# A segment-recurrent attention and its gradients: forward steps regrouped, V's rows moved by DMA, partial sums added by a matmul

## The chip, the cores and the metric

The kernel runs on one core of a Trainium2 chip. The core has a matrix engine (TensorE, PE in the profile; its weight loads are PEld), a vector engine (VectorE, DVE), a scalar engine (ScalarE, ACT), GpSimd (POOL) and a queue engine (SyncE, SP) that issues DMAs; SPq and POOLq are the DMA-issuing sides of SP and POOL. Engines run their own instruction streams in order and wait for one another by semaphores. The metric is the device time of one execution in microseconds, the median of several runs.

## The reference

The reference is a transformer block and its gradient. x is 2048 tokens of 448 numbers. The attention works through 64 segments of 32 tokens. Ahead of each segment stand 8 memory rows, which are the attention's own output for the 8 memory rows of the segment before, so segment s+1 can't start before segment s has ended:

```python
mem = mem0                                       # 8 x 448
for s in range(64):
    h = concat([mem, xs[s]])                     # 40 x 448
    q, k, v = h @ Wq, h @ Wk, h @ Wv             # 16 heads of 256
    scores = q @ k.T * scale                     # 40 x 40 per head, masked
    p = softmax(scores)
    o = (p @ v) @ Wo                             # 40 x 448
    mem = o[:8]; outs.append(o[8:])
h = x + concat(outs)                             # xs is layernorm(x)
h2 = h + (silu(n(h) @ w_gate) * (n(h) @ w_up)) @ w_down
```

The kernel returns h2 and the gradients for x, mem0, the four attention weights and the three weights of the feed-forward part. The gradient runs the recurrence backward: the gradient of `mem` goes from segment s+1 to s.

## The kernel before

The program has four stages, one after the other: a forward loop over the 64 segments (`forward_chain`), the feed-forward part with its own gradient (`ffn_phase`), a backward loop over the 64 segments (`backward_chain`), and the weight gradients (`tail_phase`). The order of instructions on each engine is the order in which the Python code states them (`manual_schedule`); no planner moves anything. Tiles wait for one another by the regions that they read and write.

**A segment's tokens.** Four segments make a tile of 128 rows. In each segment, only 32 of the 40 rows depend on the chain: the 8 memory rows and 24 of the segment's own. The other 8 of its own are computed for four segments at once in side units (`b_units` for k, q and v of the next tile, `o_units` for the output product of the tile before). The side units are cut into pieces (u1, e1, u2, u3, e3, ut, et) that stand between the pieces of the chain: `cur` is this segment's unit, `late` and `late2` hold the rest of the units of the two segments before. In every fourth segment (r = 0) `cur` is an output unit, in the others a projection unit.

**A projection** (`proj`, L468) multiplies 32 rows by 512 columns of weights, for four column groups at a time: the result of group g stands in partitions 32g to 32g+31 of one PSUM bank, 4 x 4 matmuls for a half of all columns. Kev, Qev and Vev are the copies in SBUF, [128, 1024], the first 512 columns being half 0. The evacuations alternate between DVE (`V`, L431) and ACT (`A`, L434). K and Q are then transposed (`tr_half`, L474) into kT and qT, which `scores` (L505) multiplies into two PSUM banks, s_ps0 and s_ps1, one for each half of the heads. The mask is put there ahead by a matmul (`mask_mm`, L488).

**V in rows.** P V needs V with the 40 tokens in partitions. `v_shift` copies 32 rows of each group from Vev to V_sb: DVE does half 0 and two groups of half 1, POOL (L731) the other two. The 8 rows of the side units come by DMA (`v_b_rows`, L646). V_sb holds heads 0 to 7 in partitions 0 to 39 and heads 8 to 15 in partitions 64 to 103. V_sb is stored to HBM as Vtok (L777) for the backward loop; K and Q are stored at L706 and L719.

**Softmax** runs on DVE and ACT, half by half: max (L738), subtract (L740), Exp (L742), sum (L745), reciprocal (L747), multiply into P_sb (L748). Meanwhile TensorE runs u1 and u2 of the side unit and the `spin` matmuls (L847), whose result is not used. `p_turn` (L761) transposes P head by head, 16 times 40x40; two copies, one on DVE and one on ACT, bring it to PT. Then 32 matmuls of P and V (L792), copies into oA and oB, 64 matmuls with Wo (`wo_mm`, L583) into four partition groups: group g holds a partial sum of one half of the 448 columns.

**The turn.** ACT copies the partial sums to `part`, two f32 transposes (L513) turn it, and a DVE reduce over the groups (`gsum`, L518) adds two partial sums per token and writes the next segment's memory rows into hA. A second reduce writes the segment's own rows to aT. The next segment's first projection waits for hA.

**The backward loop** ends its segment in the same way: `part` (copied half by ACT, half by DVE), a `turn` of four f32 transposes (L1207) and a `gsum` of four partial sums per token (L1212) into dA, the input of the next segment's projection. Once in four segments the side unit's partD is turned too, right behind it.

Of the kernel before, what the change touches and what calls it, by code (L numbers as in the profile page):

```python
# [15 lines left out]
P = 128  # L16
# [166 lines left out]
def run_all(k: _K):  # L183
# [38 lines left out]
    k.ident, k.identf = ident, identf  # L222
    eps_t = const.tile([P, 1], FP32)
# [38 lines left out]
    P_all = dram.tile([NSEG, 64 + L, H // 2 * L], BF16, name="P_all")  # L262
# [10 lines left out]
    with tc.tile_pool(name="wfwd", bufs=1) as wf, \  # L273
# [25 lines left out]
        with tc.tile_pool(name="workA", bufs=2) as work, tc.tile_pool(name="stageA", bufs=1) as stage:  # L299
# [22 lines left out]
            mv1 = small.tile([P, NT, 2], FP32, name="mv1", bufs=1)  # L322
# [58 lines left out]
    if True:  # L381
# [4 lines left out]
        if True:  # L386
            with tc.tile_pool(name="psB", bufs=6, space=bass.MemoryType.PSUM) as psb, \
# [6 lines left out]
                k.part = stage.tile([P, DP], FP32, name="partC")  # L394
                k.partB = stage.tile([P, DP], FP32, name="partD")
# [11 lines left out]
def forward_chain(k: _K, hA, NWIN, Wq_sb, Wk_sb, Wv_sb, Wo_sb, maskr, work, stage, ff):  # L407
# [27 lines left out]

    def slot(s):
        return s % NWIN
# [56 lines left out]
    def hsel(x, half):  # L494
        return x[0:NR].rearrange("p (a b i) n -> p a b i n", a=2, b=2)[:, :, half, :, :]
# [14 lines left out]
    def turn(src):  # L510
        y = ps1(FP32)
        for j in range(2):
            nc.tensor.transpose(y[0:DB, j * P:(j + 1) * P], src[:, j * DB:(j + 1) * DB], identf[:, :])  # L513
        return y[0:DB, 0:2 * P].rearrange("p (c b n) -> p c n b", c=KC, b=2)

    def gsum(out, in_):
        with nc.allow_low_precision("four float32 partial sums of one token"):
            nc.vector.tensor_reduce(out=out, in_=in_, axis=AX.X, op=ALU.add)  # L518
# [11 lines left out]
    def b_units(t, which):  # L530
# [6 lines left out]

        def u1():
            st["p0"] = ps1(FP32)
            proj(st["p0"], W_sb, stat, 0)  # L540
# [6 lines left out]
        def u2():  # L547
            st["p1"] = ps1(FP32)
            proj(st["p1"], W_sb, stat, 1, range(0, 2))

        def u3():
            proj(st["p1"], W_sb, stat, 1, range(2, 4))
# [33 lines left out]
    def o_units(t):  # L586
# [27 lines left out]
        def et():  # L614
            for kc in range(KC):
                gsum(T.aT[0:DB, kc, :].rearrange("p (r j) -> p r j", r=4)[:, :, XA:SEG],
                     st["y"][:, kc, :, :].rearrange("p (r i) g -> p r i g", r=4))
# [30 lines left out]

    def v_shift(V_sb, Vev, half, gs, eng):
# [15 lines left out]
    nc.gpsimd.memset(V_sb[:], 0.0)  # L665
    mask_mm(0)
# [4 lines left out]
    for s in range(NSEG):  # L671
# [19 lines left out]
        kT = work.tile([P, MC, L], BF16, name="kT", bufs=2)  # L691
        qT = work.tile([P, MC, L], BF16, name="qT", bufs=2)
# [13 lines left out]
        nc.sync.dma_start(out=dr["KtokA"][s], in_=Kev[:])  # L706
        pv0 = ps1()
        proj(pv0, Wv_sb, stat, 0)
        A(Vev[:, 0:HB], pv0[:, :])
# [3 lines left out]
        A(fm_view(kT, 0, 0, SEG), tr_half(Kev, 0))  # L713
        v_shift(V_sb, Vev, 0, (0, 1), V)
# [9 lines left out]
        pv1 = ps1()  # L724
        proj(pv1, Wv_sb, stat, 1, range(0, 2))
        A(fm_view(qT, 1, 0, SEG), tr_half(Qev, 1))
        proj(pv1, Wv_sb, stat, 1, range(2, 4))
        scores(qT, kT, 0)
        scores(qT, kT, 1)
        A(Vev[:, HB:GF], pv1[:, :])  # L730
        v_shift(V_sb, Vev, 1, (0, 1), lambda out, in_: nc.gpsimd.tensor_copy(out=out, in_=in_))  # L731
# [3 lines left out]
        P_sb = work.tile([P, HG, L], BF16, name="P_sb", bufs=2)  # L735
        for half in range(2):
# [5 lines left out]
            nc.scalar.activation(out=E_sb[0:NR, half], in_=S_sb[half][0:NR], func=ACT.Exp, scale=k.scale)  # L742
        for half in range(2):
# [8 lines left out]
        cur["u2"]()  # L752
        PT = work.tile([P, HG, L], BF16, name="PT", bufs=2)
        ppt = [ps1(BF16), ps1(BF16)]

        def p_turn(half):
            for gg in range(2):
                b = QB * gg
                for hh in range(HG):
                    if (hh // 2) % 2 == half:  # L760
                        nc.tensor.transpose(ppt[gg][b:b + L, hh * L:(hh + 1) * L], P_sb[b:b + L, hh, :], ident[b:b + L, b:b + L])  # L761
# [8 lines left out]
        for gg, eng in ((0, V), (1, A)):  # L770
            b = QB * gg
            eng(PT[b:b + L], ppt[gg][b:b + L, 0:HG * L].rearrange("p (h n) -> p h n", n=L))
        v_shift(V_sb, Vev, 1, (2, 3), V)
# [8 lines left out]
        for half in range(2):  # L782
            for gg in range(2):
                b = QB * gg
                po = ps1()
                i = 0
                for g in (2 * gg, 2 * gg + 1):
                    for j in range(4 * half, 4 * half + 4):
                        c = g * NJ + j
                        hh = c // DC - HG * gg  # L790
                        lc = c * P - gg * 2 * GF
# [1031 lines left out]
```

## Time and profile before

| | us |
|---|---|
| median of 3 runs | 3095.26 |
| lowest, highest | 3066.39, 3104.03 |
| profiled execution | 3067.6 |
| its span, first to last instruction | 3065.8 |
| forward loop, P V matmuls first to last | 70.6 to 1025.9 |
| backward loop, its products with dO first to last | 1402.4 to 2352.1 |

The busy time of an engine is the time in which it has an instruction of its own running; TensorE's matmuls overlap, so its busy time isn't its peak. A row of the timeline gives start, duration, engine, source line, operation, written tile `<-` read tiles, shape and count; what stands in brackets is the idle time before it and what ended it. The line numbers are those of the kernel before.

### The profile page before, as it was taken

Reading aid. Unit: us, or ns where it says so; the run is one execution under the profiler, and the core shown is the slowest. Engines: PE = TensorE matmul, PEld = TensorE weight load, DVE = VectorE, ACT = ScalarE, POOL = GpSimd, SP = SyncE. Lnnn points to the kernel's source line nnn. Section 1 sums busy time; section 2 is a strip of 40 time slices with the busy share of each in tenths; the row PEclk is TensorE's granted clock in tenths of the full one; section 3 lists DMA queues with packets and bytes.
Section 4 is the critical chain, followed back from the end, with each engine's and each line's share of the span. In section 5 each row is a group of like instructions: output and inputs, shape, how many; then the busy total and the mean of one; then the engine's idle time right before and its main releaser. Section 6 shows DMA issues by size and latency. Waiting matters only on the chain.

```text
span 3065.8 us, 108383 instructions
## 1 busy us (share of the span) xinstructions
PE 2825.9 (92%) x46532; PEld 1540.9 (50%) x46568; DVE 1546.5 (50%) x4123; ACT 1175.4 (38%) x3023; POOL 738.1 (24%) x1384
## 2 busy tenths in 40 slices
PE   3999999999999699995999999999998999989999
PEld 1555555555555355552555555555554454444454
DVE  4566666666655477772655566556554112211221
ACT  2444444444444356562444444444443111101110
POOL 1222222222222122221222222223222222223332
PEclk7999999999999899997999999999999999999999
DMA  8333333333333773348566566555566999999996
GB/s 262 101 103 114 114 104 108 119 104 105 107 119 99 200 181 116 117 133 188 138 183 154 143 177 158 143 169 171 138 158 197 309 222 197 197 204 208 195 208 135
DMA packets 612448, 482.84 MB, mean 157 GB/s; under 512 B 482944, under 2 KB 526544, under 8 KB 602432
## 3 DMA queue, kind: packets, MB, share of 16 engines
q1 hardware_dynamic: 565632, 289.17, 43.6%
q0 software_dynamic: 46336, 186.74, 18.3%
q8 instruction: 366, 6.00, 0.8%
q14 instruction: 114, 0.93, 0.1%
HBM read 135.08 MB, written 219.52 MB: 116 GB/s over the span
## 4 chain that ended last, share of the span: by engine, by line
PE 75%; issue 6%; DMA 5%; DVE 5%; ACT 5%; SPq 2%; POOL 1%; POOLq 0%; ACTq 0%; DVEq 0%
PE psf L468 14%; PE psf L1669 12%; PE psf L1200 10%; PE psf L1173 4%; PE psf L583 4%; PE psf L1474 3%; PE psf L1654 3%; PE psf L978 3%; PE psh L474 3%; ACT dO_sb L1167 2%; PE psf L1682 2%; PE psf L1061 2%; DMA wall<-in_A_Wv_dram 2%; PE s_ps L847 1%; PE pob L1200 1%
## 5 line engine op out<-in xcount | busy, mean ns | idle before, releaser
L468 PE MATMUL psf<-wall,hA 112*32 112x512 bf16 x6144 | 379.3, 381 | 17.0 <-DVE hA L518 15.2
L1669 PE MATMUL psf<-wall,H_all 128*128 128x512 bf16 x1404 | 320.9, 381 | 13.1 <-DMA wall<-dKA 11.0
L1669 PEld LDWEIGHTS <-H_all 128*128 128x128 bf16 x1440 | 139.5, 98 | 178.2 <-issue 21.2
L468 PEld LDWEIGHTS <-hA 112*32 112x32 bf16 x6144 | 140.5, 96 | 163.8 <-DVE hA L518 31.3
L1581 DVE CAST resc<-psf 128x512 bf16<-128x512 f32 (+1 forms) x58 | 39.1, 673 | 317.4 <-PE psf L1669 283.3
L731 POOL COPY V_sb<-Vev 32x512 bf16<-32x512 bf16 x128 | 77.6, 606 | 341.0 <-PE s_ps L505 329.9
L1579 ACT CAST resc<-psf 128x512 bf16<-128x512 f32 (+1 forms) x54 | 31.0, 574 | 329.0 <-PE psf L1669 291.6
L1525 POOL COPY dmem<-dA 128x32 bf16<-128x32 bf16 x63 | 13.3, 211 | 553.8 <-DVE dA L1212 553.8
L468 PE MATMUL psf<-wall,hB 112*32 112x512 bf16 x1536 | 105.6, 397 | 32.8 <-DMA wall<-in_A_Wk_dram 13.4
L1164 DVE COPY partC<-psf 128x224 f32<-128x224 f32 x64 | 25.1, 392 | 219.6 <-ACT partC L1167 219.6
L1173 PE MATMUL psf<-wall,dA 128*32 128x512 bf16 x2048 | 123.4, 383 | 13.0 <-DVE dA L1212 13.0
L1654 PEld LDWEIGHTS <-wall 128*128 128x128 bf16 x864 | 84.3, 99 | 90.4 <-issue 12.6
L1654 PE MATMUL psf<-dOut_all,wall 128*128 128x448 bf16 x640 | 125.7, 355 | 3.3 <-DMA wall<-OTA 3.3
L583 PE MATMUL psf<-wall,oA 128*32 128x224 bf16 x4096 | 115.5, 268 | 11.8 <-DVE oA L431 11.6
L1200 PE MATMUL psf<-wall,dkA 128*32 128x448 bf16 x2048 | 112.0, 361 | 14.3 <-DMA wall<-in_A_Wk_dram 13.0
L1164 DVE COPY dO_sb<-dOev 32x512 bf16<-32x512 bf16 x256 | 121.0, 472 | 7.1
L1200 PE MATMUL psf<-wall,dqA 128*32 128x448 bf16 x2048 | 111.1, 357 | 13.0 <-DMA wall<-in_A_Wq_dram 10.0
L1200 PE MATMUL psf<-wall,dvA 128*32 128x448 bf16 x2048 | 121.8, 357 | 0.7 <-issue 0.7
L431 DVE COPY V_sb<-Vev 32x512 bf16<-32x512 bf16 x384 | 109.4, 285 | 9.2
L1167 ACT CAST dOev<-psf 128x512 bf16<-128x512 f32 x64 | 37.5, 586 | 184.7 <-PE psf L1173 180.9
L583 PEld LDWEIGHTS <-oA 128*32 128x32 bf16 x4096 | 97.3, 99 | 19.7 <-DVE oA L431 18.4
L1200 PE MATMUL pob<-wall 128*32 128x448 bf16 x1536 | 106.4, 356 | 0.3 <-issue 0.3
(281 smaller groups left out, 5736.2 us busy)
## 6 DMA issues: line engine op xcount, KB each, us to landing
Vtok<-V_sb SPq DMA_DIRECT2D x128, 192.0 KB
KtokA<-Kev SPq DMA_DIRECT2D x64, 256.0 KB
QtokA<-Qev SPq DMA_DIRECT2D x64, 256.0 KB
OTA<-oA POOLq DMA_DIRECT2D x16, 1024.0 KB
Q_sb<-QtokA SPq DMA_DIRECT2D x128, 128.0 KB
K_sb<-KtokA SPq DMA_DIRECT2D x128, 128.0 KB
dVA<-dvA POOLq DMA_DIRECT2D x16, 1024.0 KB
dKA<-dkA POOLq DMA_DIRECT2D x16, 1024.0 KB
```

What stands on the lines that cost most here:

```text
L431: nc.vector.tensor_copy(out=out, in_=in_)
L468: nc.tensor.matmul(ps[32 * g:32 * g + 32, :], lhsT=stat(kc), rhs=W_sb[0:DB, kc, c0:c0 + HB], start=(kc == 0), stop=(kc == KC - 1))
L474: nc.tensor.transpose(pt[:, j * P:(j + 1) * P], ev[:, half * HB + j * P:half * HB + (j + 1) * P], ident[:, :])
L583: nc.tensor.matmul(ps[32 * g:32 * g + 32, 0:2 * DB], lhsT=x, rhs=Wo_sb[:, c, a * 2 * DB:(a + 1) * 2 * DB], start=first, stop=last)
L978: nc.tensor.matmul(out[b][:, 0:BW], lhsT=xT[:, kc, :], rhs=Wx[:, kc, f0:f0 + BW], start=(kc == 0), stop=False)
L1164: nc.vector.tensor_copy(out=out, in_=in_)
L1167: nc.scalar.copy(out=out, in_=in_)
L1173: nc.tensor.matmul(ps[32 * g:32 * g + 32, :], lhsT=stat(kc), rhs=WoT_sb[:, kc, c0:c0 + HB], start=(kc == 0), stop=(kc == KC - 1))
L1200: nc.tensor.matmul(pO[32 * g:32 * g + 32, 0:D], lhsT=ch(c), rhs=WT[:, c, :], start=(first and i < 4), stop=(last and i >= MC - 4), skip_gr ...
L1474: nc.tensor.matmul(po[:, n * L:(n + 1) * L], lhsT=lhs[b:b + L, lc:lc + P], rhs=rhs[b:b + L, hh, :], start=True, stop=True)
L1654: nc.tensor.matmul(ps[:, 0:D], lhsT=stat[:, i, c * P:(c + 1) * P], rhs=Y[:, i, 0:D], start=(i == 0), stop=(i == kts - 1))
L1669: nc.tensor.matmul(ps[:, 0:N], lhsT=Hx[:, i, dc * P:(dc + 1) * P], rhs=X[:, i, b * N:(b + 1) * N], start=(i == 0), stop=(i == kts - 1))
```

## The change

In the forward loop:

- The order of the projections is K, K, Q, Q, then all four transposes, V half 0, the scores, and V half 1 behind the scores.
- V's columns are projected in another order (`proj_v`), so that partitions 0 to 39 of V_sb hold the even heads and 64 to 103 the odd ones. P_sb is padded to 64 columns a head, so that a transpose turns two heads (104x128) at once: four transposes for sixteen. PT is block-diagonal for a pair of heads, with zeros set once, and a matmul of P and V takes both heads: 16 matmuls of 80 columns for 32 of 40.
- Turned P is copied by four ACT copies, each of 40x160, for one of 40x320 on DVE and one on ACT.
- V's rows of half 0 are moved by four SP DMAs, issued ahead of the stores of K and Q; of half 1, three groups by DVE behind the softmax and one by ACT. POOL moves none.
- The `spin` matmuls are gone; u3 of the side unit stands between the two halves of P V.
- kT and qT have one buffer instead of two.

In both loops `turn` multiplies the f32 `part` by a f32 matrix of zeros and ones (`sel2`, `sel4`), which turns it and adds the partial sums in one step; a DVE copy replaces `gsum`. P goes to HBM and back with its padding (1024 instead of 640 bytes a row), and the backward loop takes V's transposed columns in the new order.

```diff
@@ the constants
+    for a in range(2):
+        nc.vector.tensor_tensor(out=sel2[:, 32 * a:32 * a + 32], in0=identf[:, 64 * a:64 * a + 32],
+                                in1=identf[:, 64 * a + 32:64 * a + 64], op=ALU.add)
+    nc.vector.tensor_tensor(out=sel4[:], in0=sel2[:, 0:32], in1=sel2[:, 32:64], op=ALU.add)
@@ forward_chain
+    def proj_v(ps, stat, half, kcs=range(4)):
+        for kc in kcs:
+            wv = Wv_sb[0:DB, kc, :].rearrange("p (x y f e d) -> p x y f e d", x=2, y=2, f=2, e=2)
+            for g in range(G):
+                e, x = divmod(g, 2)
+                nc.tensor.matmul(ps[32 * g:32 * g + 32, :].rearrange("t (y d) -> t y d", y=2), lhsT=stat(kc),
+                                 rhs=wv[:, x, :, half, e, :], start=(kc == 0), stop=(kc == KC - 1))
...
-            nc.tensor.transpose(y[0:DB, j * P:(j + 1) * P], src[:, j * DB:(j + 1) * DB], identf[:, :])
-        return y[0:DB, 0:2 * P].rearrange("p (c b n) -> p c n b", c=KC, b=2)
+            nc.tensor.matmul(y[0:DB, j * 64:(j + 1) * 64], lhsT=src[:, j * DB:(j + 1) * DB], rhs=k.sel2[:, :],
+                             start=True, stop=True)
+        return y[0:DB, 0:P].rearrange("p (c n) -> p c n", c=KC)
...
-        pv0 = ps1()
-        proj(pv0, Wv_sb, stat, 0)
-        A(Vev[:, 0:HB], pv0[:, :])
         pq0 = ps1()
         proj(pq0, Wq_sb, stat, 0)
         V(Qev[:, 0:HB], pq0[:, :])
-        A(fm_view(kT, 0, 0, SEG), tr_half(Kev, 0))
-        v_shift(V_sb, Vev, 0, (0, 1), V)
         pq1 = ps1()
         proj(pq1, Wq_sb, stat, 1)
         A(Qev[:, HB:GF], pq1[:, :])
-        V(fm_view(kT, 1, 0, SEG), tr_half(Kev, 1))
-        nc.sync.dma_start(out=dr["QtokA"][s], in_=Qev[:])
+        V(fm_view(kT, 0, 0, SEG), tr_half(Kev, 0))
+        A(fm_view(kT, 1, 0, SEG), tr_half(Kev, 1))
         V(fm_view(qT, 0, 0, SEG), tr_half(Qev, 0))
-        v_shift(V_sb, Vev, 0, (2, 3), V)
+        V(fm_view(qT, 1, 0, SEG), tr_half(Qev, 1))
...
+        pv0 = ps1()
+        proj_v(pv0, stat, 0)
+        A(Vev[:, 0:HB], pv0[:, :])
+        v_shift(V_sb, Vev, 0, range(4), D_)
+        nc.sync.dma_start(out=dr["KtokA"][s], in_=Kev[:])
+        nc.sync.dma_start(out=dr["QtokA"][s], in_=Qev[:])
         scores(qT, kT, 0)
         scores(qT, kT, 1)
+        pv1 = ps1()
+        proj_v(pv1, stat, 1)
...
+        A(Vev[:, HB:GF], pv1[:, :])
...
+        v_shift(V_sb, Vev, 1, (1, 2, 3), V)
         cur["u1"]()
         cur["e1"]()
...
-        spin(k, S_ps[0], 2)
-        p_turn(0)
-        spin(k, S_ps[1], 1)
         if s + 1 < NSEG:
             mask_mm(0)
             mask_mm(1)
+        p_turn(0)
+        p_ev(0, 0, A)
+        p_ev(0, 1, A)
+        v_shift(V_sb, Vev, 1, (0,), A)
+        cur["u2"]()
         p_turn(1)
-        cur["u3"]()
+        p_ev(1, 0, A)
+        p_ev(1, 1, A)
...
         for half in range(2):
+            if half == 1:
+                cur["u3"]()
             for gg in range(2):
...
+                for i in range(2):
+                    for dc in range(DC):
+                        c0 = gg * GF + half * HB + i * Dh + dc * P
+                        nc.tensor.matmul(pw[:, i, :, dc, :], lhsT=V_sb[0:NR, c0:c0 + P],
+                                         rhs=PT[0:NR, half, 2 * gg + i, :].rearrange("p (e n) -> p e n", e=2),
                                          start=True, stop=True)
...
-            gsum(hA[0:DB, :, slot(s + 1), 0:M], y[:, :, 0:M, :])
-        gsum(T.aT[0:DB, :, r * SEG:r * SEG + XA], y[:, :, M:SEG, :])
+            V(hA[0:DB, :, slot(s + 1), 0:M], y[:, :, 0:M])
+        V(T.aT[0:DB, :, r * SEG:r * SEG + XA], y[:, :, M:SEG])
@@ backward_chain
-            nc.tensor.transpose(y[:, kc * P:(kc + 1) * P], src[:, c0:c0 + P], identf[:, :])
-        return y[:, 0:DP].rearrange("p (c g n) -> p c n g", c=KC, g=G)
+            nc.tensor.matmul(y[:, kc * SEG:(kc + 1) * SEG], lhsT=src[:, c0:c0 + P], rhs=k.sel4[:, :], start=True, stop=True)
+        return y[:, 0:KC * SEG].rearrange("p (c n) -> p c n", c=KC)
...
-            gsum(dA[:, :, slot(s - 1), 0:M], y[:, :, 0:M, :])
+            V(dA[:, :, slot(s - 1), 0:M], y[:, :, 0:M])
```

`D_` is `nc.sync.dma_start`; `p_ev(half, e, eng)` copies one diagonal block of turned P.

More of the change, by code (lines that the diff above doesn't have):

```diff
@@ L393, in run_all @@
                 nc.vector.memset(k.s_ps[:], 0.0)
-                k.part = stage.tile([P, DP], FP32, name="partC")
-                k.partB = stage.tile([P, DP], FP32, name="partD")
+                k.part = stage.tile([P, D], FP32, name="partC")
+                k.partB = stage.tile([P, D], FP32, name="partD")
                 if True:
@@ L536, in stat, with mm @@
             return T.hB[0:DB, kc, :, :]
+        def mm(ps, half, kcs=range(4)):
+            if which == "v":
+                proj_v(ps, stat, half, kcs)
+            else:
+                proj(ps, W_sb, stat, half, kcs)
         def u1():
             st["p0"] = ps1(FP32)
-            proj(st["p0"], W_sb, stat, 0)
+            mm(st["p0"], 0)
         def e1():
@@ L665, in forward_chain @@
     nc.gpsimd.memset(V_sb[:], 0.0)
+    Ps, PTs = [], []
+    for i in range(2):
+        Ps.append(work.tile([P, HG // 2, P], BF16, name=f"P_sb{i}", bufs=1))
+        nc.gpsimd.memset(Ps[i][:], 0.0)
+        PTs.append(work.tile([P, 2, 4, 2 * L], BF16, name=f"PT{i}", bufs=1))
+        nc.gpsimd.memset(PTs[i][:], 0.0)
     mask_mm(0)
@@ L749, in forward_chain, with p_ev @@
                                     in1=hview(rs[half][0:NR].unsqueeze(2).to_broadcast([NR, HQ, L])), op=ALU.mult)
+        v_shift(V_sb, Vev, 1, (1, 2, 3), V)
         cur["u1"]()
         cur["e1"]()
[L752 to L753 removed]
+        PT = PTs[s % 2]
         ppt = [ps1(BF16), ps1(BF16)]
         def p_turn(half):
[L757 to L761, printed above, removed]
[L762 to L764 removed]
+            for i in range(2):
+                nc.tensor.transpose(ppt[half][:, i * P:i * P + NR], P_sb[0:NR, 2 * i + half, :], ident[0:NR, 0:NR])
+        def p_ev(half, e, eng):
+            eng(PT[QB * e:QB * e + L, half, :, e * L:(e + 1) * L].rearrange("p (g a) n -> p g a n", g=2),
+                ppt[half][QB * e:QB * e + L, 0:2 * P].rearrange("p (a g n) -> p g a n", a=2, g=2)[:, :, :, 0:L])
         if s + 1 < NSEG:
@@ L841, in forward_chain @@
     out_ev(NT - 1)
-def spin(k, ps, n, reps=4):
-    x = k.ident[:, :].unsqueeze(1).to_broadcast([P, reps, P])
-    for _ in range(n):
-        k.nc.tensor.matmul(ps[:, 0:reps * P], lhsT=k.ident[:, :], rhs=x, start=True, stop=True, skip_group_check=True)
 def _get_small(k):
```

78 lines of the change are left out of this document (30 added, 48 removed).

## The prediction

> **What bounds the kernel now.** I read the page first, then busy time by stage, then the timeline of one forward and one backward segment. The page says that TensorE carries the span:
>
> ```profile
> PE 2825.9 (92%) x46532; PEld 1540.9 (50%) x46568; DVE 1546.5 (50%) x4123; ACT 1175.4 (38%) x3023; POOL 738.1 (24%) x1384
> PE 75%; issue 6%; DMA 5%; DVE 5%; ACT 5%; SPq 2%; POOL 1%; POOLq 0%; ACTq 0%; DVEq 0%
> ```
>
> The second line is the chain that ended last. The change touches two stages, the forward loop (its matmuls of P and V run from 70.6 to 1025.9 us) and the backward loop (1402.4 to 2352.1), 64 segments each; each segment needs the result of the one before. A forward segment repeats every 15.05 us (DVE starts the reduce into hA at 603.68, 618.73, 633.78), a backward one about every 14.29 (1907.42, 1921.71). What counts is therefore the chain inside one segment. The timeline of the forward segment whose first projection starts at 619.01 (columns: start, duration, engine, line, operation, tiles):
>
> ```profile
> 625.86 0.75 PE L505 MATMUL s_ps<-kT,qT 128*40 128x40 bf16 x32
> 626.39 0.33 DVE L738 TENSOR_REDUCE mx<-s_ps 104x4 f32<-104x160 f32 x1 [0.63 <-PE s_ps L505]
> 628.94 0.32 DVE L748 TENSOR_TENSOR P_sb<-E_sb,rs 104x160 bf16<-104x160 f32 x1
> 629.69 0.42 ACT L434 COPY PT<-psh 40x320 bf16<-40x320 bf16 x1 [1.17 <-PE psh L761]
> 630.08 0.82 PE L792 MATMUL psf<-PT,V_sb 40*128 40x40 bf16 x32
> 630.61 0.76 DVE L431 CAST oA<-psf 128x256 bf16<-128x256 f32 x2
> 631.09 1.72 PE L583 MATMUL psf<-wall,oA 128*32 128x224 bf16 x64 [0.19 <-DVE oA L431]
> 632.92 0.35 ACT L434 COPY part<-psf 128x224 f32<-128x224 f32 x1 [1.37 <-PE psf L583]
> 633.32 0.43 PE L513 MATMUL psf<-identf,part 128*112 128x128 f32 x2
> 633.78 0.23 DVE L518 TENSOR_REDUCE hA<-psf 112x32 bf16<-112x64 f32 x1 [2.15 <-PE psf L513]
> ```
>
> TensorE is busy nearly throughout, but part of it is padding: work after the scores only fills the softmax wait. Counted from 619.01, the scores start at 6.85, the softmax ends at 10.25, the Wo product starts at 12.08 and the next segment at 15.05. In the backward segment the end is the same kind of chain:
>
> ```profile
> 1920.31 0.35 ACT L1167 COPY partC<-psf 128x224 f32<-128x224 f32 x1 [2.52 <-PE psf L1200]
> 1920.68 0.39 DVE L1164 COPY partC<-psf 128x224 f32<-128x224 f32 x1 [2.88 <-ACT partC L1167]
> 1920.71 0.97 PE L1207 MATMUL psf<-identf,partC 128*128 128x128 f32 x4
> 1921.71 0.29 DVE L1212 TENSOR_REDUCE dA<-psf 128x32 bf16<-128x128 f32 x1 [0.64 <-PE psf L1207]
> ```
>
> **Scores earlier.** V's second half (16 projection matmuls, 0.98 us in the timeline) moves from before the scores to behind them, and transposes stop alternating with projections. Four projections end at 3.57, as before (L468 x64). Sixteen transposes in a row: a group of 4 alone takes 0.33, a group of 8 takes 0.55, so 0.33 + 3 x 0.22 = 0.99, to 4.56; the last group needs Q's second half, copied by ACT from 3.69 to 4.28. V's first half: 0.98, to 5.54. Scores at **5.54 instead of 6.85**, if the copies of qT follow: 0.44 after a transpose group starts, 0.42 each on DVE, the last ends about 5.3. The first reduce comes 0.53 later (626.39 - 625.86), P's halves 2.07 and 2.87 after that start: 8.14 and 8.94. The 0.98 of V, 0.98 of the side unit and 0.28 of the mask now fill this wait; the three `spin` matmuls (0.60 + 0.39) go with it. Their removal is counted at nothing for the clock: the granted clock is 1.00 from 500 to 900 us, and also from 1600 to 1700, where the backward has no such filler and is busy 94.26 of 100 us.
>
> **From P to Wo.** ACT is now the longest queue. After the second Exp (1.65 behind the first reduce, 7.72) come V's second half (0.59), the side unit's copy (0.57; not in every fourth segment), two copies of turned P (40x160; between the rows 0.42 for 40x320 and 0.22 for 128x64, I take 0.30; ends 0.22 and 0.42), V's row move (0.62, the ACT row of the same 32x512 copy in the backward), and two more copies: 8.33, 8.92, 9.56, 10.20, 10.84. DVE makes its three row moves (3 x 0.285) from 8.94 and is done by 9.8. So "fewer copies" holds for columns, not for instructions: two copies of 320 become four of 160.
>
> V's first-half rows go by DMA. No row shows a 32x1KB move inside SBUF; the nearest is the 8-row move, issued four times in 2.77 us, with the bytes of the last two visible in slices of 0.1 us from 652.5 on:
>
> ```profile
> 650.81 2.77 SPq L646 DMA_DIRECT2D V_sb<-bevv  x4
> GB/s 102 62 41 123 61 21 0 0 0 0 102 41 21 0 0 0 0 102 41 21 143 369 369 369 410 389 389 185 0 0 143 389 369 451 389 348 389 144 0 0
> ```
>
> They pass at 653.5 and 654.2 while the last issue began near 652.9: 0.69 per issue, about 1.55 to land. Ends for an issue: 0.33 (QtokA's) and 0.69; I take 0.69, the same kind of move. Vev is ready at 6.30 (5.71 + 0.59), the issues start at 6.37, 7.06, 7.75, 8.44, the last lands at 9.99. P times V half 0 starts at 9.62 (turned P), its second group waits for that DMA, 10.05 to 10.2; u3 (0.55) to 10.77; half 1 waits for ACT's 10.84, 16 products instead of 32, about 0.32 for its eight (40 columns are 0.025 apart, 128-column transposes 0.056; I take 0.04). Wo starts at **11.25 instead of 12.08**; without the side unit's copy 11.0. Mean gain (3 x 0.83 + 1.08)/4 = 0.89 a segment. Behind the V moves SP holds the K and Q stores (issue near 9.2; their buffers are rewritten only after 15) and Vtok's; the next segment's V tail rows wait for Vtok and end some 1.5 us into it, well before 6.37.
>
> **The sum products.** Two f32 transposes and a reduce become two f32 matmuls against a 0/1 matrix and a plain copy (backward: four). The copies: 0.23 to about 0.20 and 0.29 to about 0.20 (128x64 casts take 0.215). No row shows an f32 matmul that isn't a transpose. Starts of f32 transposes (128 columns) are 0.11 apart, of bf16 ones 0.056: four-byte operands already cost double. Lower end: half the columns with one weight load, no dearer than now, 0.03 to 0.05 saved each. Upper end: four weight loads each, 0.33 more. I take two loads, 0.11 more: a product, unlike a copy through the array, must use both halves of the stationary. Then forward: 4 loads instead of 2, +0.22, less half the columns, **+0.165**; backward, for the three behind DVE's partC: 6 instead of 3, **+0.25**. Once in four backward segments the side unit's partD (0.60 now) stands between turn and the next projection; with 8 loads (0.88) it ends some 0.6 later than the copy that it stood beside. The Trainium skill ("FP8 and Floating Point Precision", TensorE Precision Notes) says that true FP32 takes four passes through the array. With the weights held through them, four passes of 64 columns would be the 256 columns that a doubled 128 already cost, and the sum would be that of the lower end; with a load each it is the upper end; the trace of before can't say.
>
> **At nothing:** memsets of padded P and PT on POOL (2304 columns; V_sb's 2048 took 1.83, so 2.1 us, beside the first tile's projections; uncovered, 2.1 once); single kT/qT (POOL's tail copies run at 619.24 to 619.99, five us before the scores); wider P rows in HBM (its readers take the same columns, 0.49 an operation); the freed reduces of aT and dxnT, off the chain.
>
> **Sum.** Forward: 63 x (-0.89 + 0.165 - 0.03) = -47.6. Backward: 63 x (0.25 - 0.09) = +10.1, partD 15 x 0.6 = +9. Total -28.5. The profiled execution (3067.6, span 3065.8) becomes 3039; the median of the runs lies 27.7 higher, so **3067** in its terms. The runs spread 1.2%, so 2% is about what can be told from no change.
>
> **Rivals.** (1) *Sum products cost no more than transposes.* For it: half the columns, fewer PSUM columns to read. Forward 63 x (-0.89 - 0.03 - 0.05) = -61, backward 63 x (-0.09 - 0.05) = -9: -70, 3025. (2) *Slower: four weight loads per f32 product,* in the turn at each segment's end, where nothing covers it. Forward four loads more than in the forecast, +0.605 a segment; backward six more, +0.91; partD 16 loads, 1.76, some 0.25 of it beside the copy, +1.5: 63 x (-0.89 - 0.03 + 0.605) + 63 x 0.82 + 15 x 1.5 = -20 + 52 + 23 = +55, 3150. It decides from three loads per product; at two the forward gain still wins. For it: f32 already doubles; against: forward's two products are short. (3) *V's DMA becomes the wait.* If the last row move lands at 11.0 instead of 9.99 (slower issue with 32 rows, or stores in the same rings), u3 and half 1 follow it and Wo starts at 12.1: the forward gain is gone, -28.5 + 56 = +27, 3122. Each 0.1 past 10.1 costs 6. (4) *The scores don't come earlier,* because ACT's or DVE's copies hold them: against it, the walk leaves 0.2.
>
> **Chances.** Forecast 0.46 (alone 3045 to 3090), (1) 0.2, (2) 0.14, (3) 0.14, (4) and the rest 0.06. The range from 3008, rival 1 in an execution as quick as the profiled one, to 3130, past rival 3, leaves out most of rival 2. Faster by over 2% (under 3033) is most of rival 1 and a little of the forecast, 0.18; slower by over 2% (above 3157) the upper half of rival 2, also with 3, 0.14; within, 0.68.
>
> **What would show it.** Right: reduces into mx 6.0 to 6.2 after a segment's first projection; a period near 14.3; P-V matmuls released by ACT's copy of turned P; the turn rows with two loads per product and about 0.6 (forward). Wrong: P-V matmuls waiting for V_sb's DMA (rival 3); turn rows with one load (1) or four (2); qT copies ending after 5.6 (4); a granted clock under 1.00 in the forward, which nothing above prices.

## The result and the profile after

The changed kernel takes 3124.66 us (median; 3109.03 to 3149.43), the kernel before 3079.34 us (3065.83 to 3104.03) beside it on the same chip. The ratio is **1.016**, with a 95% interval of 1.0135 to 1.0185: 1.6% slower, less than the 2% bound, where 0.9% faster was forecast. The time lies inside the stated range of 3008 to 3130; the direction is wrong. The profiled execution of the changed kernel took 3140.96 us with a span of 3139.2, the one before 3067.6 with a span of 3065.8: +73.4, where the medians differ by 45.3. The one is among the longer of its fifteen executions, the other among the shorter, so the traces show the change larger than it is in the median. Each stage time in this document is that of one execution. Times between the reduces or copies into hA (forward) and dA (backward) split the +73.4: first segment's work +2.0, forward +42.4 (936.3 to 978.7 over 62 periods), feed-forward part +2.9, backward +24.9 (906.6 to 931.5), tail +1.2. So the backward came out near its forecast of +19, and the forward went wrong: +42 instead of -48.

The page of the changed kernel, its busy times and the chain that ended last:

```profile
PE 2851.0 (91%) x45064; PEld 1618.7 (52%) x45064; DVE 1459.4 (46%) x3838; ACT 1218.8 (39%) x3215; POOL 659.3 (21%) x1260
...
PE 70%; DMA 8%; SPq 7%; issue 6%; ACT 6%; DVE 1%; POOL 1%; another core or an unknown queue 0%; ACTq 0%; POOLq 0%; DVEq 0%
PE psf L1685 12%; PE psf L1220 10%; PE psf L478 8%; PE psf L604 5%; DMA V_sb<-Vev 4%; PE psf L1193 4%; SPq L670 4%; PE psf L1490 3%; PE psf L1670 3%; PE psf L1227 3%; PE psf L998 3%; PE psf L486 2%; ACT dO_sb L1187 2%; PE psh L492 2%; PE psf L1698 2%
```

The chain has two members that it didn't have: the DMA `V_sb<-Vev`, 4%, and SP's issuing of it (L670), another 4%. PE's share fell from 75 to 70%. TensorE's waits (total us, times, longest) name the same tile at the head of the list; in the kernel before, the matmuls of P and V (L792) wait 2.5 us in all, 0.9 of it for a DMA. First the changed kernel, then the one before:

```profile
PE psf L818 <- DMA V_sb<-Vev: 60.2, 84, 7.7
PE psf L1490 <- ACT dO_sb L1187: 20.5, 61, 0.3
```

```profile
PE psf L792 <- DVE PT L431: 1.6, 4, 0.4
PE psf L792 <- DMA V_sb<-bevv: 0.9, 2, 0.6
```

The stretches of the forward loop in the changed kernel (columns: stretch, its length, then busy time of PE, PEld, DVE, ACT and POOL, granted TensorE clock, DMA share, GB/s):

```profile
100.00:500.00 400.00, 363.30 (x7264) 217.00 (x7259) 214.10 (x670) 198.22 (x518) 54.97 (x132) 0.96 0.37 115
500.00:900.00 400.00, 360.61 (x6936) 215.76 (x6940) 204.96 (x635) 186.74 (x486) 54.97 (x132) 0.92 0.36 112
```

And of the kernel before:

```profile
100.00:500.00 400.00, 384.68 (x8299) 213.37 (x8295) 243.44 (x790) 185.46 (x455) 91.60 (x196) 1.00 0.36 110
500.00:900.00 400.00, 385.72 (x8245) 212.21 (x8239) 245.27 (x795) 185.80 (x449) 89.47 (x190) 1.00 0.35 107
```

TensorE is idle 21 to 25 us longer per 400 us, and its clock is no longer 1.00. In the whole forward the clock stands at half for 106.5 us in 26 of 62 segments; before it was 7.5 us in 3 segments at the loop's two ends (1, 61 and 62). The segments are cut here from write to write of hA; the expectations below speak of 29.

**One segment that goes as the walk said, and one that doesn't.** The timeline of the changed kernel, a segment whose first projection starts at 907.26:

```profile
912.89 0.74 PE L523 MATMUL s_ps<-kT,qT 128*40 128x40 bf16 x32
913.42 0.33 DVE L763 TENSOR_REDUCE mx<-s_ps 104x4 f32<-104x160 f32 x1 [0.89 <-PE s_ps L523]
913.67 2.43 SPq L670 DMA_DIRECT2D V_sb<-Vev  x4
...
916.93 0.30 PE L818 MATMUL psf<-PT,V_sb 104*128 104x80 bf16 x4 [0.27 <-PE psh L784]
917.60 0.30 PE L818 MATMUL psf<-PT,V_sb 104*128 104x80 bf16 x4 [0.37 <-DMA V_sb<-Vev]
918.77 1.72 PE L604 MATMUL psf<-wall,oA 128*32 128x224 bf16 x64
```

Counted from 907.26: scores at 5.63, first reduce at 6.16, four DMA issues in 2.43 us from 6.41, P times V at 9.67, Wo at 11.51. The second group of P times V waits 0.37 for the DMA; the period is 14.57. The segment from 598.61:

```profile
604.24 0.74 PE L523 MATMUL s_ps<-kT,qT 128*40 128x40 bf16 x32
605.02 3.60 SPq L670 DMA_DIRECT2D V_sb<-Vev  x4
...
609.47 0.30 PE L818 MATMUL psf<-PT,V_sb 104*128 104x80 bf16 x4 [1.46 <-DMA V_sb<-Vev]
610.33 0.30 PE L818 MATMUL psf<-PT,V_sb 104*128 104x80 bf16 x4 [0.56 <-DMA V_sb<-Vev]
611.12 0.46 PE L818 MATMUL psf<-PT,V_sb 104*128 104x80 bf16 x8
611.51 3.08 PE L604 MATMUL psf<-wall,oA 128*32 128x224 bf16 x64
615.82 0.19 DVE L438 CAST hA<-psf 112x32 bf16<-112x32 f32 x1 [3.66 <-PE psf L531]
```

Up to the scores it is the same. Then the four issues take 3.60 instead of 2.43, P times V starts at 10.86, Wo at 12.90, and Wo itself takes 3.08 instead of 1.72. The clock explains the last: the same stretch in windows of 3.41 us (columns as above):

```profile
604.83:608.24 3.41, 3.18 (x57) 1.28 (x51) 3.14 (x12) 2.62 (x8) 0.29 (x1) 1.00 0.10 24
608.24:611.66 3.42, 1.63 (x32) 1.00 (x36) 0.95 (x4) 1.34 (x5) 0.26 (x1) 1.00 0.78 242
611.66:615.08 3.42, 3.42 (x70) 2.86 (x63) 0.50 (x3) 0.90 (x4) 0.00 (x0) 0.50 0.28 84
615.08:618.49 3.41, 3.33 (x61) 1.97 (x62) 2.57 (x7) 1.54 (x3) 1.39 (x4) 1.00 0.10 33
```

TensorE was busy for 1.63 of 3.42 us; for the next 3.41 us it got half a clock, just while Wo ran. What stood beside the slow issues is in the DMA view of 605 to 608.7 (queue, packets, MB, share of 16 engines):

```profile
q1 hardware_dynamic: 104, 0.07, 7.8%
q8 instruction: 1, 0.02, 2.2%
```

A packet on q8 is 16384 bytes of instructions: 356 of them for 91,172 recorded instructions of TensorE (matmuls, weight loads and its sequencer's), so 256 instructions each; in all nine kernels 256 times the packets comes within 0.2% of these. The one here starts 0.6 us after the first issue began. In the undisturbed segment the same view has none between 912.9 and 916.5.

### The profile page after: what moved, and what is told of

It reads as the page before. It is cut to its first block, busy times and chain, and to the rows that moved or that the text cites. A ratio compares the mean times of both kernels' runs of the same rounds, so it can differ in the third digit from the quotient of the medians.

```text
span 3139.2 us, 105729 instructions
## 1 busy us (share of the span) xinstructions
PE 2851.0 (91%) x45064; PEld 1618.7 (52%) x45064; DVE 1459.4 (46%) x3838; ACT 1218.8 (39%) x3215; POOL 659.3 (21%) x1260
## 4 chain that ended last, share of the span: by engine, by line
PE 70%; DMA 8%; SPq 7%; issue 6%; ACT 6%; DVE 1%; POOL 1%; another core or an unknown queue 0%; ACTq 0%; POOLq 0%; DVEq 0%
PE psf L1685 12%; PE psf L1220 10%; PE psf L478 8%; PE psf L604 5%; DMA V_sb<-Vev 4%; PE psf L1193 4%; SPq L670 4%; PE psf L1490 3%; PE psf L1670 3%; PE psf L1227 3%; PE psf L998 3%; PE psf L486 2%; ACT dO_sb L1187 2%; PE psh L492 2%; PE psf L1698 2%
## 5 line engine op out<-in xcount | busy, mean ns | idle before, releaser
L478 PE MATMUL psf<-wall,hA 112*32 112x512 bf16 x4096 | 235.1, 382 | 14.8 <-DVE hA L438 13.6
L478 PEld LDWEIGHTS <-hA 112*32 112x32 bf16 x4096 | 104.1, 97 | 123.6 <-DVE hA L438 24.0
L818 PE MATMUL psf<-PT,V_sb 104*128 104x80 bf16 x1024 | 74.2, 213 | 79.9 <-DMA V_sb<-Vev 60.2
L604 PE MATMUL psf<-wall,oA 128*32 128x224 bf16 x4096 | 141.7, 305 | 0.0
L486 PE MATMUL psf<-wall,hA 112*32 112x512 bf16 x2048 | 134.0, 382 | 0.0
L801 POOL DMA_DIRECT2D P_all<-P_sb x64 | 35.2, 550 | 458.6 <-DVE P_sb L774 440.3
L604 PEld LDWEIGHTS <-oA 128*32 128x32 bf16 x4096 | 114.4, 113 | 13.2
L818 PEld LDWEIGHTS <-V_sb 104*128 104x128 bf16 x1024 | 50.6, 105 | 121.6 <-issue 74.8
```

What stands on the lines that cost most here:

```text
L478: nc.tensor.matmul(ps[32 * g:32 * g + 32, :], lhsT=stat(kc), rhs=W_sb[0:DB, kc, c0:c0 + HB], start=(kc == 0), stop=(kc == KC - 1))
L486: nc.tensor.matmul(ps[32 * g:32 * g + 32, :].rearrange("t (y d) -> t y d", y=2), lhsT=stat(kc), rhs=wv[:, x, :, half, e, :], start=(kc == ...
L604: nc.tensor.matmul(ps[32 * g:32 * g + 32, 0:2 * DB], lhsT=x, rhs=Wo_sb[:, c, a * 2 * DB:(a + 1) * 2 * DB], start=first, stop=last)
L818: nc.tensor.matmul(pw[:, i, :, dc, :], lhsT=V_sb[0:NR, c0:c0 + P], rhs=PT[0:NR, half, 2 * gg + i, :].rearrange("p (e n) -> p e n", e=2), s ...
```

## The experiments

Theory A, formed from these rows: the V moves have no slack, an instruction fetch beside them makes their issue or landing late, TensorE idles, and the idle time costs a clock window. Against it stands above all B: the clock falls because the `spin` filler is gone, whatever V does. The new softmax wait and the sum products could slow the forward too.

**V's first half moved by POOL instead of DMA.**

```diff
-        v_shift(V_sb, Vev, 0, range(4), D_)
+        v_shift(V_sb, Vev, 0, range(4), G_)
```

> The changed kernel with one line other: the four row moves of V's first half are POOL copies (32x512, 0.61 each in the kernel before, 2.4 in all, from about 6.4 to 8.8 after the first projection) instead of SP's DMAs. Theory A, the DMA lands late and the idle time then lets the clock fall: every forward segment repeats in 14.36 to 14.5 (as the undisturbed ones of the changed kernel do), matmuls of P and V start near 9.6, nearly no half-clock windows between segments 2 and 58 (29 segments had one), the 62 periods sum to about 894 instead of 978.7, and the time falls by 60 to 85, to 3040 to 3065. Theory B, the clock falls because the spin matmuls are gone, whatever the moves: the half-clock windows stay (20 or more), mean period 15.2 or more, time 3090 to 3115. Theory C, POOL's copies beside the softmax slow DVE: the reduce-to-P_sb chain takes longer than 2.9.

Measured: 3062.81 us (3046.68 to 3087.14), ratio to the kernel before 0.996 (0.9924 to 0.9995), within what theory A expected. The forward takes 892.5 instead of 978.7, its typical period is 14.32, and half-clock is left only in the last two segments, which have no side units. Its windows:

```profile
100.00:500.00 400.00, 379.76 (x7905) 227.75 (x7898) 243.28 (x722) 216.21 (x559) 128.83 (x258) 1.00 0.36 117
500.00:900.00 400.00, 380.00 (x7897) 228.04 (x7895) 245.15 (x728) 216.51 (x560) 129.50 (x259) 1.00 0.36 116
```

There is no `spin` here either, and the clock is 1.00: B falls as a cause by itself, and with it any cause that sits in the softmax wait or the forward's turn. By these two executions the four DMAs cost 86 us of the forward more than the POOL copies.

Theory C holds as well: from the first reduce to P_sb the softmax takes 3.28, in the changed kernel 2.87. One operation makes the difference, the multiply into P_sb (min/median/max ns), first here, then in the changed kernel:

```profile
L774 DVE TENSOR_TENSOR P_sb<-E_sb,rs x128: 324/426/735, 70.6 to 981.8; 104x160 bf16<-104x160 f32 x128
L774 DVE TENSOR_TENSOR P_sb<-E_sb,rs x128: 324/325/327, 70.6 to 1066.2; 104x160 bf16<-104x160 f32 x128
```

The first half's multiply, which runs beside POOL's copies, has a median of 0.73. So POOL's moves cost something too, 0.4 us ahead of the matmuls of P and V.

**The `spin` matmuls back, DMAs kept.** Three products of 512 columns, as many as the kernel before had, ahead of the mask:

```diff
+        spin(k, S_ps[0], 2)
+        spin(k, S_ps[1], 1)
         if s + 1 < NSEG:
             mask_mm(0)
             mask_mm(1)
```

> The changed kernel with the three spin matmuls (128x512 each, about 0.21 apart) back, ahead of the mask and of P's transposes; V's first half still by DMA. Theory A: the waits for V_sb's DMA stay as they are, matmuls of P and V start 9.5 to 10.9 after the first projection as now, but 0.65 of the idle time before them is filled; half-clock windows fall from 29 segments to under 10, which gives back 1.7 each, some 35 to 50: 3075 to 3090. Theory B: all half-clock windows of the forward go, 50 to 55. If instead the clock depends on the single long gap rather than on the sum of work, the windows stay and the time is within 10 of the changed kernel's.

Measured: 3099.33 us (3088.25 to 3112.89), ratio 1.0074 (1.0047 to 1.0101), more than expected. Half-clock went from 26 segments to 5, though P times V still waits for the DMA, 24.1 us instead of 60.2:

```profile
PE psf L820 <- DMA V_sb<-Vev: 24.1, 30, 8.5
```

So lateness and clock come apart: the issues are still stretched in 25 segments, and with the idle time filled they hardly cost a clock window. The filler costs 0.3 us itself, though, since P's transposes stand behind it: an undisturbed period is 14.77 instead of 14.45 (medians). It gives back 41 us of the forward (937.6), half of what the POOL moves give.

**The turn of before (f32 transposes and reduces) in both loops.** The edit, here for the backward; the forward's and the copies into hA, dA, aT and dxnT go with it:

```diff
-            nc.tensor.matmul(y[:, kc * SEG:(kc + 1) * SEG], lhsT=src[:, c0:c0 + P], rhs=k.sel4[:, :], start=True, stop=True)
+            nc.tensor.transpose(y[:, kc * P:(kc + 1) * P], src[:, c0:c0 + P], identf[:, :])
```

> The changed kernel with the old turn in both loops: f32 transposes against the identity and a reduce on DVE instead of f32 products and a copy. If the products cost two weight loads each (the trace of the changed kernel has four loads for two products): the backward loop's 62 periods sum to about 906 instead of 931.5, the forward's undisturbed period falls by 0.1 to 0.15 to about 14.25, the time falls by 30 to 40, to 3085 to 3095. Rival: the backward's growth comes from the wider rows of P or V's new order, then its periods stay at 931 and only the forward's 9 us come back.

Measured: 3099.99 us (3081.12 to 3112.33), ratio 1.0042 (1.0011 to 1.0074), just above what was expected. The backward's typical segment went from 14.80 to 14.60, the value of before, its sum from 931.5 to 920.7; some 906 had been expected. Part of that miss is the clock, which stood at half for 23.5 us in this backward, 9.6 in that of before: worth about 7 us. Nearly all of the 14 us above the kernel before sit in every fourth segment (mean 15.98, before 15.05); the others are within 0.02 of it. Why is not explained, so the rival of wider P rows or V's new order is not excluded for this part. The forward (950.5) kept its trouble, half-clock in 21 segments: the sum products are not its cause. Its undisturbed period fell from 14.45 to 14.32, as expected.

**Both together** (POOL moves and the old turn).

```diff
-        v_shift(V_sb, Vev, 0, range(4), D_)
+        v_shift(V_sb, Vev, 0, range(4), G_)
...
-            nc.tensor.matmul(y[:, kc * SEG:(kc + 1) * SEG], lhsT=src[:, c0:c0 + P], rhs=k.sel4[:, :], start=True, stop=True)
+            nc.tensor.transpose(y[:, kc * P:(kc + 1) * P], src[:, c0:c0 + P], identf[:, :])
```

> Both of the two edits before: V's first half moved by POOL copies and the old turn. If the two causes are separate their gains add: 3000 to 3030, 1.5 to 2.5 per cent under the kernel before. If the half-clock windows come from the missing spin, the same sum without the clock's part: 3060 to 3080.

Measured: 3030.44 us (3026.58 to 3040.4), ratio 0.9848 (0.981 to 0.9885), at the upper edge of what was expected. Forward 883.0, backward 915.3. With POOL's moves as base, the sum products cost 9.5 us in the forward and 21.8 in the backward.

**Half of the dose: two groups by DMA, two by POOL.**

```diff
-        v_shift(V_sb, Vev, 0, range(4), D_)
+        v_shift(V_sb, Vev, 0, (0, 1), D_)
+        v_shift(V_sb, Vev, 0, (2, 3), G_)
```

> The changed kernel with half of the dose: of V's first-half row moves, groups 0 and 1 stay DMAs on SP's queue, groups 2 and 3 are copied by POOL, as all four were in the run with POOL's moves. Theory A (each DMA takes 0.54 to 0.59 us of issue, an instruction fetch beside it stretches the issues by up to 1.3 us for four of them, and there was no slack left): two issues from about 6.4 us after a segment's first projection end near 7.6, the last row lands about 8.6, with a fetch beside it at most about 9.7; the matmuls of P and V start at 9.7 as with POOL's moves, hardly any of them waits for the DMA, half-clock windows in the forward in 0 to 6 segments instead of 26, forward near 900 us (978.7 in the changed kernel, 892.5 with POOL's moves), total near 3070. Theory D (it is not the number of issues: a DMA that meets a fetch is late whatever is ahead of it): waits for V_sb's DMA stay in about 20 segments, forward 930 to 970, total 3090 to 3115.

Measured: 3046.83 us (3040.69 to 3061.55), ratio 0.991 (0.9878 to 0.9942). The forward is 882.0, the period 14.07: better than theory A's own 900. Its waits and windows:

```profile
PE psf L819 <- DMA V_sb<-Vev: 10.9, 14, 4.8
```

```profile
100.00:500.00 400.00, 384.64 (x7962) 232.34 (x7954) 234.93 (x734) 216.22 (x565) 96.27 (x205) 1.00 0.38 122
500.00:900.00 400.00, 384.96 (x8023) 232.55 (x8016) 236.20 (x736) 217.08 (x570) 95.68 (x204) 1.00 0.39 124
```

Half-clock is left in 3 segments. Fetches start between 6.3 and 9.4 us in 34 segments, 36 in the changed kernel, but two issues end some 1.15 us earlier than four (two times 0.57 by this kernel's row of L670), and that much is left for a slow one. A DMA that meets a fetch is therefore not late as such (theory D), though single issues still take up to 1.70; it is late when nothing is left to absorb it. P times V starts at 9.38 here and at 9.72 with four POOL copies. The softmax makes that difference: POOL's two copies end at 7.85, before the multiply into P_sb, which takes 0.325 again, and the chain from the first reduce to P_sb 2.87.

**The fetches pushed to other places.** That the fetch stretches the issues was so far an observation: in the changed kernel the four issues' durations add up to over 2.6 us in 29 segments, and 28 of these have a fetch that starts 6.4 to 8.6 us after the first projection. This run moves the fetches and nothing else, by 128 PE instructions ahead of the loop:

```diff
+    for i in range(64):
+        nc.tensor.matmul(S_ps[0][0:32, 0:32], lhsT=ident[:, 0:32], rhs=ident[:, 0:32], start=True, stop=True,
+                         skip_group_check=True)
     mask_mm(0)
     mask_mm(1)
```

> The changed kernel with 64 small matmuls (32 columns, overwritten by the mask, about 4 us in all) ahead of the forward loop, nothing else: TensorE's instruction stream is shifted by 128 instructions, half of what one 16384-byte instruction fetch holds, so that the fetches fall at other places of each segment. In the changed kernel's trace the issues of the four V moves are stretched (over 2.6 us in all instead of 2.30) in 29 of 62 segments: of segments s with s mod 4 = 1 in 5 to 37, of those with s mod 4 = 2 in 6 and 18 to 50, s mod 4 = 3 in 39 to 59, s mod 4 = 0 in 8, 48, 56, 60. Theory A1 (the fetch beside the moves is the cause): the stretched segments become others, and again those whose fetch starts 6.3 to 8.5 us after the first projection; the pattern drifts by some 11 instructions per four segments, so a shift of 128 moves it by about 12 groups of four: s mod 4 = 1 free from 1 to about 45, s mod 4 = 2 free from about 6, s mod 4 = 3 stretched in 3 to 15, s mod 4 = 0 stretched in most from 12 to 52; some 15 to 25 in all; total 3090 to 3140. Theory A2 (something that repeats with the segment's own work, a store or a load of a neighbour, stretches them, and the fetch only happens to stand there): the same segments as before are stretched.

Measured, segments with issues over 2.6 us in all:

| s mod 4 | changed kernel | shifted by 128 instructions |
|---|---|---|
| 1 | 5, 9, 13, 17, 21, 25, 29, 33, 37 | 49, 53, 57, 61 |
| 2 | 6, 18, 22, 26, 30, 34, 38, 42, 46, 50 | 2, 6, 46 |
| 3 | 39, 43, 47, 51, 55, 59 | 3, 7, 11, 15, 19, 23, 27 |
| 0 | 8, 48, 56, 60 | 8, 12, 16, 20, 24, 28, 36, 44 |

Only 6, 46 and 8 are in both columns. The shifted kernel has 22 such segments, each with a fetch that starts 6.6 to 8.2 us after the first projection, and half-clock in 16; its forward takes 953.7, and the one execution 3129.57. The pattern is where the theory put it, but for its ends: s mod 4 = 3 runs on to 27 instead of 15, and s mod 4 = 0 ends at 44 (in 32, 40, 48 and 52 the fetch starts at 8.7 to 9.0, when the issues are nearly over). The segment's own stores and loads, which the edit leaves in place, aren't what stretches the issues. Over the four kernels with four DMAs (this, the changed one, `spin`, old turn) the issues are stretched in 103 of 112 segments with a fetch in that window, and in 2 of 136 without; these two have one that starts just ahead of it, at 6.0 and 6.2.

**Two DMAs and the old turn.**

```diff
-        v_shift(V_sb, Vev, 0, range(4), D_)
+        v_shift(V_sb, Vev, 0, (0, 1), D_)
+        v_shift(V_sb, Vev, 0, (2, 3), G_)
...
-            nc.tensor.matmul(y[:, kc * SEG:(kc + 1) * SEG], lhsT=src[:, c0:c0 + P], rhs=k.sel4[:, :], start=True, stop=True)
+            nc.tensor.transpose(y[:, kc * P:(kc + 1) * P], src[:, c0:c0 + P], identf[:, :])
```

> The two repairs together: of V's first-half row moves two groups by DMA and two by POOL, as in the run before, and the f32 transposes with their DVE sums back in both loops. If the two costs simply add: the forward gives 882 less what the old turn was worth with POOL's moves (892.5 to 883.0, so 9.5), 872; the backward 915 to 921, as in the two runs with the old turn; the total against the kernel before near 0.978 to 0.982, 3010 to 3030 us. If the forward with two DMAs is no longer bound by the chain through the sum products (the DVE reduce would then collide with other DVE work), it stays at 882 and the total at 3025 to 3040.

Measured: **3019.16 us** (3015.06 to 3028.22), ratio 0.9811 (0.9762 to 0.986): 1.9% faster than the kernel before and the lowest of the versions, though its interval overlaps that of POOL's moves with the old turn. Forward 866.9, less than the 872 expected, backward 916.0. The costs add, within 6 us. Its page:

```profile
span 3015.0 us, 104843 instructions
...
PE 2761.2 (92%) x44548; PEld 1534.2 (51%) x44584; DVE 1504.0 (50%) x3934; ACT 1219.2 (40%) x3215; POOL 738.7 (25%) x1388
```

## Why the prediction was wrong

**Right: scores earlier.** 5.54 was worked out, 5.63 measured; the first reduce falls at 6.16, inside the 6.0 to 6.2.

**Right, where the rows come in time: from P to Wo.** Wo was put at 11.25, 11.0 without the side unit's copy. The median is 11.27 with POOL's moves, 11.01 with two DMAs, and 11.4 in the changed kernel's segments without a fetch beside the moves. That 11.27 meets the number is luck, since it holds the 0.4 us of slower softmax; the two-DMA kernel shows that the walk was some 0.2 too slow. Of that, ACT's last copy of turned P is the main part: it ends at 10.58 in an undisturbed segment, and 10.84 was worked out. The forecast forward change of -47.6 us, sum products included, is about what those two kernels have: -43.8 and -54.3. The gain was there to be had; V's DMAs took it back.

**Wrong: the V moves as a fixed time.** The step "the issues start at 6.37, 7.06, 7.75, 8.44, the last lands at 9.99" fits the undisturbed segments: issues start at 6.41, 2.30 us for four, the last row passes at 9.8 to 9.9. It allowed 0.1 to 0.2 of slack and took one duration for each of 64 segments. There was no slack even where nothing disturbs them: the second group of P times V starts at 10.23 in these segments, behind the DMA, and at 9.63 with two DMAs, and Wo starts 0.39 later. The bounds of an issue were 0.33 and 0.69; measured is 0.53 to 1.89, by the page of the tile:

```profile
L670 SPq DMA_DIRECT2D V_sb<-Vev x256: 529/590/1887, 68.4 to 1065.7; - x128
```

The kernel before already showed a spread for the 8-row moves that were used for the price, and one value was taken:

```profile
L646 SPq DMA_DIRECT2D V_sb<-bevv x252: 624/631/1702, 76.4 to 1017.6; - x126
```

It also showed an issue stretched beside a packet of instructions: QtokA's store took at most 0.46 without one (50 issues), up to 1.38 with one (14).

Rival 3 named this wait, with other causes (more rows, stores in the same rings). That its 3122 lies near the result is luck: it was +27 on a median of 3095.26, which fifteen runs put at 3079.34, and measured is +45. Its account was another one, too: a late row in each segment, 0.9 each. What the runs show is a late row in about half of the segments, and mostly another price.

**Wrong, and the larger part: "Their removal is counted at nothing for the clock."** The reason given was that the clock was 1.00 where TensorE was busy nearly all the time. That shows nothing of a kernel in which it must wait. In the changed kernel's forward the segments divide like this (mean period):

| | segments | period us | over 14.52 |
|---|---|---|---|
| issues in time, full clock | 25 | 14.52 | |
| issues stretched, full clock | 11 | 15.01 | 5.4 |
| issues in time, half clock in it | 8 | 16.56 | 16.3 |
| stretched, half clock in it | 18 | 17.68 | 56.9 |

The last column is segments times the excess, 78.6 us together, which is the forward's 978.7 less 62 x 14.52. Three of the eight segments of the third row (1, 61 and 62) lie at the loop's ends, where the kernel before loses its clock too. Being late alone costs 0.5 us a segment; being late with the clock lost costs 3.2. In the changed kernel the `spin` matmuls work as cover, not as idle padding (half-clock in 5 segments with them, in 26 without); whether the kernel before needed them no run shows. The change took away the cover and made the rows late at once. Where V comes in time the cover isn't needed (POOL moves, two DMAs: clock 1.00 without any `spin`), so "at nothing" holds only together with rows in time. The prediction did list a clock under 1.00 as what would make it wrong, and priced it nowhere.

**Right: two weight loads per sum product.** For 64 segments with two and four products each, the groups of L531 and L1227 have 256 and 512 loads (min/median/max in ns):

```profile
L531 PEld LDWEIGHTS psf<-sel,part x256: 172/178/310, 77.5 to 1079.9; 128*112 128x112 f32 x128
```

```profile
L1227 PEld LDWEIGHTS psf<-sel,partC x512: 186/192/192, 1485.8 to 2436.2; 128*128 128x128 f32 x171
```

Rivals 1 (one load) and 2 (four) are out. The Trainium skill ("FP8 and Floating Point Precision", TensorE Precision Notes) has four passes for true FP32; here the trace shows two loads and two matmuls for each product, so the time went by neither of the two readings that were weighed, four held passes or four loads. The end of a backward segment in the changed kernel:

```profile
1910.00 1.28 PE L1227 MATMUL psf<-sel,partC 128*128 128x32 f32 x8
1911.32 0.19 DVE L1184 CAST dA<-psf 128x32 bf16<-128x32 f32 x1 [0.95 <-PE psf L1227]
```

The products take 1.28 us where the transposes took 0.97, so +0.31; the copy takes 0.19 where the reduce took 0.29. +0.25 less 0.09 was forecast, +0.20 on the typical segment is measured (14.60 to 14.80). In one segment of four, where partD stands between, the typical growth is 0.74, so 0.54 more; 0.6 was forecast. The backward's sum of +24.9 for a forecast of +19 is a size a little low, the clock's part in it small (13.7 us at half instead of 9.6). Taking the products out again gave 10.8, 21.8 and 16.1 us in the three pairs of runs. In the forward they cost 9.5 and 15.1 in the pairs with full clock (10.4 was in the sum, 63 x 0.165, less 1.9 for the copy).

**Hidden as forecast:** parts outside the two loops moved by +2.0, +2.9 and +1.2 us.

**A sum that doesn't come out:** the range's lower end of 3008 is said to be rival 1 in an execution as quick as the profiled one, but 3067.6 less rival 1's 70 is 2998.

## What to carry to other kernels

A DMA on a recurrent path needs slack for its slowest issue, not its median one: two moves by DMA with a microsecond to spare, and two by POOL, were worth 97 us of forward (978.7 to 882.0) against four by DMA with none. An engine that takes over such work can slow another beside it: look for the price there too, as with POOL's four copies and the softmax. Before a filler of TensorE is taken out, ask what happens to the clock in the segment where the wait behind it runs long; price the filler and the late case together. And a stage that is late in some segments only is found by a table by segment, with what differs between them, rather than by the mean of the loop.

## What the runs showed of the hardware

**An instruction fetch slows the issue of 32x1KB DMAs beside it.** TensorE's stream comes in packets of 16384 bytes on a DMA queue of its own, 256 instructions each, and 0.9 to 1.7 us long in the forward. When one starts during four 32x1KB moves inside SBUF, these take about 3.0 us to issue (means 2.96 to 3.05 in four kernels) instead of 2.3, up to 3.6. Where they are stretched in the changed kernel, the last row passes at 10.1 to 11.4, 0.3 to 1.6 us late. By single issues of that kernel: 168 without a packet beside them took at most 0.61, 88 with one up to 1.89. Not every slow issue has this cause: of the 8-row moves of V's tail in the same kernel, 40 of 193 without a packet beside them took over 0.76, and 4 of 59 with one; why is open. The place of the fetch drifts through the segments by some 11 instructions in four segments, since these have 2293 recorded PE instructions and nine packets hold 2304, so a loop of equal segments has unequal times. Whether the packet holds up the issuing or the rings was not separated.

**POOL's copies slow one DVE operation beside them.** In the two kernels with four POOL copies, the first half's multiply into P_sb takes 0.73 and 0.72 (medians) instead of 0.325. The subtract, the sum and the reciprocal beside the same copies keep their times (0.325, 0.307 and 0.178). Why only the multiply is slowed stays open.

**The clock falls on a part-busy window.** Over the forward loops of all nine kernels, in steps of 3.413 us on the grid that the clock's records have, with the clock at 1.00:

| TensorE busy in the step, us | steps | followed by half clock |
|---|---|---|
| under 1.9 | 41 | 41 |
| 1.9 to 2.3 | 45 | 30 |
| 2.3 to 2.5 | 24 | 5 |
| 2.5 to 2.8 | 83 | 1 |
| over 2.8 | 2137 | 0 |

By the table the limit lies between 1.9 and 2.5 us, some two thirds of the step, and the loss mostly lasts 3.41 us (75 of the 87 half-clock steps were followed by full clock). The Trainium skill ("TensorE: Matmul & The Clock Gate", What's actually happening) has a free-running window of 3413 ns, which these records agree with, and lets the clock fall after an idle window; here no step that half clock followed was idle throughout: the longest gap in each was 0.5 to 1.8 us. This is read from the traces; no run set the busy share on purpose.

**Still open:** the backward with the old turn stays 9 to 14 us above that of the kernel before in sum, with a typical segment that is no longer (14.45 to 14.60). Half-clock time that is 7 to 15 us longer there accounts for 4 to 8 of it. In the two runs with DMAs the excess sits in every fourth segment (means 15.98 and 15.76, before 15.05). For the rest, and for why the clock falls more often, no run was made.
